# Query copies on VectorE, and two block pairs of tiles 3 to 6 by seven products, in an attention and feed-forward kernel

## The chip, the cores and the metric

The kernel runs on one core of one Trainium2 chip. The metric is the device time of one execution in microseconds (us), the median over several runs. Engines: TensorE (PE, its weight loads PEld), VectorE (DVE), ScalarE (ACT), GpSimd (POOL) and SyncE (SP).

## The reference

Attention with two kinds of mask, 8 batches, 8 heads, 576 positions, head size 64, then a bilinear feed-forward over all 4608 tokens of 512 features:

```python
scores = (1.0 / np.sqrt(D)) * np.matmul(q, k.transpose(0, 1, 3, 2))
rel = pos[:, None] - pos[None, :]
mask_local = (rel >= 0) & (rel < 32)
mask_strided = (rel >= 0) & (pos[None, :] % 32 == pos[:, None] % 32)
# heads 0-3 take mask_local, heads 4-7 mask_strided; masked scores are -1e9
attn = softmax(scores); o = np.matmul(attn, v)
x = o.transpose(0, 2, 1, 3).reshape(4608, 512)
out = ((x @ w_a) * (x @ w_b)) @ w_out        # w_a, w_b: 512 x 1536, w_out: 1536 x 512
```

## The kernel before, in words

**Feed-forward.** The 4608 tokens are nine tiles `t` = 0 to 8 of 512 tokens. A tile has 16 slots. Slots 0 to 11 are the blocks `f` of 128 of the 1536 inner features (`ffn_ab`): four matmuls of 512 columns for a = x @ w_a, four for b = x @ w_b (`ab_mm`, L612), a copy of a from PSUM by ScalarE (L633), and the product a * b by VectorE into `pf` (L636). Slots 12 to 15 are the y part, the multiplication with w_out. From tile 1 on it runs by seven products instead of eight (`products`, L816), whose sums of `pf` VectorE makes beforehand (`fast_s`, L750, called `ps`). The activations `xT` are a ring of four batches of 576 columns; in tile 4 the ring's end falls in the middle of the tile, and its matmuls are cut into two of 256 columns.

**Block pairs by seven products.** Seven products of half-size blocks give the four quarters of a (two feature blocks by two token halves) that eight would otherwise give. Before the change this is done for a in five pairs of tile 7 and six of tile 8 (`FAST_A`, `a_pair`), a pair being blocks 2g and 2g+1; b stays ordinary. A product is two matmuls of 256 columns (L689). Products 1, 6, 5 and 3 add up, one after the other, in one PSUM bank X; after each, ScalarE copies X into one quarter of a (L705, L708, L716, L724). Bank Z holds products 7 and 4, bank Y product 2, and they are added to the quarters by VectorE or GpSimd. The matmuls of b (L696) stand between the products. Sums of weights (`wsum_make`, L653) and differences of x (`xsum_make`, L663) are made beforehand by VectorE, the weight sums in tile 6.

**Attention.** It runs one tile ahead: batch b's steps are handed out over the slots of tile b-1 by tables (`STEPS` for batches 1 and 2, `LATER` and `IN_Y` for 3 to 7); a position of .5 is in the middle of a slot, between a and b. Each batch has eight units u, two for each of four pairs of heads c: units 0 to 3 are local heads, 4 to 7 strided heads.
- `Q`: copies the transposed queries `qT` of one half of the partitions j into the zero-padded query tile `qz` (`step_Q`, L333 strided, L335 local; GpSimd). Q0 and Q1 are the local heads, Q2 and Q3 the strided ones. `step_D` issues the transposing DMAs into `qT` on SyncE's queue.
- `S`: score matmuls (`S_p`, L377), exponential on ScalarE (L397), mask on VectorE (`S_m`, L415).
- `V`: output matmuls into the PSUM tile `o` of two banks. For the local heads (`V_p`, L454) VectorE takes reciprocals and scales (L462, L480); for the strided ones (`step_VT`, L513) ScalarE takes logarithm and exponential (L523, L524) and VectorE scales into `xT` (L527).
- `O`, `I`: the local heads' outputs go to DRAM and come back transposed into `xT`.

**Order.** Each engine's order is the program's order, written out by hand: a slot's matmuls, copy and product, then `take(i)`, the attention steps of the position, then `at[i]`, the other work put down for the slot with `do` (loads, sums, transposes). Ahead of `at[i]`, GpSimd copies one element of the slot's result (`pace`, L1054), so that the loads it issues keep pace.

**PSUM.** Eight banks: two for scores `st`, two for `o`, three `mm` and one `tp`, which `mm_bank` hands out in turn to the blocks and the y part.

Of the kernel before, what the change touches and what calls it, by code (L numbers as in the profile page):

```python
# [7 lines left out]
F32 = mybir.dt.float32  # L8
BF16 = mybir.dt.bfloat16
I16 = mybir.dt.int16  # L10
ALU = mybir.AluOpType
# [14 lines left out]
WCH = (0, 2, 5, 9, 12)  # L26
FAST_Y = (1, 2, 3, 4, 5, 6, 7, 8)
FAST_A = {7: (1, 2, 3, 4, 5), 8: (0, 1, 2, 3, 4, 5)}


@with_exitstack
def kernel(
# [34 lines left out]
    def open_psum(stack, **bufs):  # L67
        for nm, n in bufs.items():
# [7 lines left out]

    qz_pair = [(const.tile([128, 2, 2, S], BF16, name=f"qz{i}l"), const.tile([128, 2, RS, 2, NP], BF16, name=f"qz{i}s"))
               for i in range(2)]
    qz_buf = [[(l[:, :, j], s[:, :, :, j]) for j in range(2)] for l, s in qz_pair]
    qz_flat = [[l.rearrange("p a b c -> p (a b c)"), s.rearrange("p a b c d -> p (a b c d)")] for l, s in qz_pair]  # L80
# [29 lines left out]
    def fill_v(t):  # L110
        nc.gpsimd.memset(t[:, :, :, D:] if len(t.shape) == 4 else t[:, :, D:], 1.0)

# [65 lines left out]
    tl = {}  # L178

    def blocks(nm, z):  # L180
        z = int(z)
        return sb.tile([128, 2, (S, RS * GP)[z]], BF16, tag=f"t{nm}{z}", name=f"t{nm}{z}", bufs=1)

# [142 lines left out]
    def step_Q(b, z, j):  # L326

        r = slice(64 * j, 64 * j + 64)
        src = qT[z][r]
        if z:  # L330
            src = src.rearrange("d (c h p i) -> d c h i p", c=2, h=2, i=4)
            for c in range(2):
                nc.gpsimd.tensor_copy(qz_buf[b % 2][j][1][r, c].rearrange("d (h i) p -> d h i p", h=2), src[:, c])  # L333
        else:
            nc.gpsimd.tensor_copy(qz_buf[b % 2][j][0][r], src)  # L335

# [21 lines left out]
    def S_p(b, u):  # L358
# [5 lines left out]
        if b > 0:  # L364
            sv = st.rearrange("p a (i n) -> p (a i) n", n=256)
            for i in range(G):
                k0 = (G * half + i) * (LW if c < 2 else GP)
                if c < 2:
                    rhs = qz_pair[b % 2][0][:, c % 2, :, k0:k0 + n]
                else:  # L370
                    rhs = qz_pair[b % 2][1][:, c % 2, G * half + i]
                if c < 2 or b < FIRST_D:
                    lhs = kT[:, c % 2, k0:k0 + 128]
                else:
                    k0 = W * (u - HL) + i
                    lhs = kT_strided(b)[:, k0:k0 + 509:4]
                nc.tensor.matmul(sv[:, i, :2 * n].rearrange("p (j n) -> p j n", j=2), lhsT=lhs, rhs=rhs, start=True, stop=True)  # L377
            return
# [48 lines left out]
    def V_p(b, u):  # L427
# [11 lines left out]
        else:  # L439
            o = psum4["o"].tile([128, 2, 512], F32, tag="o", name="o")  # L440
            of = o[:, :, :G * (D + 1)].rearrange("p j (g e) -> p j g e", e=D + 1)
            sm = of[:, :, :, D:]
# [59 lines left out]
    def step_VT(b, u):  # L502

        c, half, M, n, G = unit(u)
        p = ps.pop((b, u))
        o = psum4["o"].tile([128, 2, 512], F32, tag="o", name="o")
        for i in range(G):
            for j in range(2):
                if c < 2:
                    vt = vl_buf[b % 2][:, (2 * c + j) * 6 + 3 * half + i]  # L510
                else:
                    vt = vs_buf[b % 2][:, u - HL, 2 * i + j]
                nc.tensor.matmul(o[:, j, i * n:(i + 1) * n], lhsT=vt, rhs=p_cols(b, p, j, i, n, n)[:M], start=True, stop=True)  # L513
# [40 lines left out]
    def step_X(b, c):  # L554
# [17 lines left out]
                 12.6: "S1", 12.75: "L0 X2", 13: "s2 X3 V0 m2 L1 W3", 13.5: "V1 S3", 14: "V2 X0", 14.5: "V3", 15: "X1"},  # L572
             2: {16.5: "Q0 Q1", 20: "S0 Q2", 20.5: "S1", 21: "V0 Q3", 21.5: "S2", 22: "V1", 22.5: "S3 O0", 23: "V2", 23.5: "S4",
                 24: "V3 I0 O1", 24.5: "S5", 25.5: "V4", 26: "S6", 26.5: "I1", 27: "V5", 27.5: "S7", 28.5: "V6", 30: "V7"}}
    LATER = {-6: "Q0", -5: "Q1", -1: "S0", 0: "S1", 1: "V0 Q2", 2: "S2", 3: "V1 O0 Q3", 4: "S3 I0", 5: "V2", 6: "S4", 7: "V3 O1", 8: "S5", 9: "V4 I1",
             10: "S6",
# [38 lines left out]
    def ffn_ab(t, f, mid, ab=None):  # L615
        if f == 0:
            pfs[t] = fsb.tile([128, FD, TTOK], BF16, tag="pf", name="pf", bufs=1)
        pf = pfs[t]
        if f // 2 in FAST_A.get(t, ()):
            if f % 2 == 0:  # L620
                pairs[t, f // 2] = a_pair(t, f // 2)
            return next(pairs[t, f // 2])
        if ab is None:
# [6 lines left out]
            else:  # L630
                ab_mm(t, f, ab, range(KD), mid)
        a_sb = fsb.tile([128, TTOK], F32, tag="a_sb", name="a_sb")
        nc.scalar.copy(a_sb, ab[0])  # L633
# [3 lines left out]
        else:  # L637
# [3 lines left out]
    wav = wa_sb.rearrange("p (j c) (g e m) -> p j c g e m", c=2, e=2, m=128)  # L641
    wsum_a = [flat.rearrange("p (c g m) -> p c g m", c=2, g=FG)
              for flat in [vl_buf[0].rearrange("p a b -> p (a b)")[:, 12 * 128 * z:12 * 128 * (z + 1)] for z in range(2)]
              + [t[:, :12 * 128] for t in qz_flat[0]]]
    xsum = {t: qz_flat[1][t - 7][:, :8 * HT].rearrange("p (n c m) -> p n c m", n=4, c=2)
            for t in FAST_A}

    def wsum_make(n):
        w, s_ = (lambda e, j: wav[:, j, :, :, e]), wsum_a
        a, b, op = ((w(1, 0), w(1, 1), ALU.add), (s_[0], w(0, 0), ALU.subtract), (w(0, 0), w(1, 0), ALU.subtract),  # L650
                    (w(0, 1), s_[1], ALU.subtract))[n]
        for c in range(2):
            nc.vector.tensor_tensor(s_[n][:, c], a[:, c], b[:, c], op=op)  # L653

    def x_part(t, j, k):
        x0 = TTOK * t % (XR * S) + HT * k
        return xT[:, 2 * j:2 * j + 2, x0:x0 + HT]
# [7 lines left out]
    pairs = {}  # L665

    def a_pair(t, g):

        pf = pfs[t]
        pool, nm = ((pst, "st"), (psum4["o"], "o"))[g % 2]  # L670
        X = pool.tile([128, 2, 512], F32, tag=nm, name="ax")[:, 0, :HT]
        a = ([fsb.tile([128, TTOK], F32, tag="a_sb", name="a_sb") for _ in range(2)] if g % 2 == 0 else
             [t.rearrange("p h n -> p (h n)")[:, :2 * TTOK].bitcast(F32) for t in kT_buf[0]])
# [62 lines left out]
    later = {}  # L736

    pss = {}

# [88 lines left out]
    def y_tail(t):  # L828

        plan, y = products(t), y_bufs()  # L830
        banks = {("X", 1): psum4["o"].tile([128, 2, 512], F32, tag="o", name="end")[:, 0, :HN],
                 ("Z", 1): pst.tile([128, 2, 512], F32, tag="st", name="end")[:, 0, :HN]}
# [74 lines left out]
    with tc.manual_schedule(engines={ENG.PE, ENG.SP, ENG.Pool, ENG.DVE, ENG.Activation}):  # L907
# [71 lines left out]
        early.close()  # L979
        open_psum(ctx, mm=3, tp=1, o=1)  # L980
        slots = []
        for t in range(NT):
# [22 lines left out]
        for b in range(FIRST_D, B):  # L1005
            g0 = 16 * (b - 2)
            if b == FIRST_D:
                do(0, load_qk, b, False)
                do(1, load_qk, b, True)
                do(15, load_vl, b)  # L1010
                for h in range(HL):
# [10 lines left out]
        for n in range(4):  # L1022
            do(16 * (NT - 3) + 2 * n + 2, wsum_make, n)
        do(16 * (NT - 2) - 1, xsum_make, NT - 2, 0)
# [8 lines left out]
        for i, jz in ((14, (0, 0)), (14, (1, 0)), (15, (0, 1)), (15, (1, 1))):  # L1033
            do(i, zero_qz, 0, nc.gpsimd, (jz,))
        do(28, fill_v, vs_buf[1])
        for n, slot in enumerate((16, 16, 19, 20)):
# [51 lines left out]
```

## Time and profile before

| | before |
|---|---|
| median of 3 runs | 326.83 us (326.56 to 326.98) |
| the profiled execution | 326.64 us |
| its span, first to last instruction | 324.9 us |
| TensorE busy | 315.5 us, 97% of the span |
| VectorE busy | 234.1 us, 72% |
| ScalarE busy | 186.4 us, 57% |
| GpSimd busy | 150.1 us, 46% |
| tile 3, 128.3 to 161.7 us: TensorE, VectorE, ScalarE, GpSimd busy | 33.24, 24.26, 19.92, 16.65 us |
| one a copy, 128x512 (L633) | 585 ns, 84 of them |
| one product a * b, 128x512 (L636) | 684 ns, 74 of them |
| one query copy on GpSimd: local 64x1152 (L335); strided, half of it (L333) | 1.15 us median, 12 of them; 0.70 us, 24 of them |

The span is the time on the core; the rest of an execution's time lies around it. A matmul's own duration includes the way through the array, so matmuls that follow each other overlap: 512 columns last 379 ns, and the next starts 216 ns later. What a stretch costs TensorE is read from the starts. In a timeline row the columns are: start, duration, engine, line, operation, written tile <- read tiles, shape, count, and in brackets the idle time before it and what ended that.

### The profile page before, as it was taken

The page shows a single profiled execution, that of the slowest core. Times are in us where ns is not written, and L with a number is a line of the kernel's source. Part 1 is how long each engine was busy: PE and PEld are TensorE (multiplying, and loading weights), DVE is VectorE, ACT ScalarE, POOL GpSimd, SP SyncE. Part 2 cuts the span into 40 slices and gives each one's busy share as a digit, 9 for nine tenths or more (in the row PEclk, how much of TensorE's full clock was granted, in tenths as well). Part 3 has the DMA queues.
Part 4 walks back from the last instruction along what each step waited for, and adds up shares of the span by engine and source line. Part 5 has one row for each costly group of instructions (what it writes and reads, how often), then busy time and mean ns, then how long its engine had stood idle before and what let it go on. Part 6 is the DMA issues. An engine that isn't in the chain of part 4 may idle for free.

```text
span 324.9 us, 7111 instructions
## 1 busy us (share of the span) xinstructions
PE 315.5 (97%) x2706; PEld 214.2 (66%) x2734; DVE 234.1 (72%) x489; ACT 186.4 (57%) x331; POOL 150.1 (46%) x240
## 2 busy tenths in 40 slices
PE   8999999998999999999999999999999999999994
PEld 6754555454765578556999995559555866786684
DVE  6765786498956785688667766777699667857862
ACT  6763766454754476447644765467546655535541
POOL 8944922893785356524652565336124003202520
PEclk9999999999999999999999999999999999999998
DMA  8999999999699999999998999999863030004004
GB/s 150 155 204 196 204 187 204 204 126 175 87 132 153 191 129 101 131 207 167 102 104 181 158 107 107 158 182 112 59 101 103 2 113 17 3 2 129 0 3 129
DMA packets 127234, 40.40 MB, mean 124 GB/s; under 512 B 115040, under 2 KB 124320, under 8 KB 127008
## 3 DMA queue, kind: packets, MB, share of 16 engines
q0 software_dynamic: 80400, 19.28, 64.5%
q1 hardware_dynamic: 46656, 20.61, 36.3%
q8 instruction: 21, 0.34, 0.5%
q14 instruction: 13, 0.11, 0.1%
q10 hardware_dynamic: 144, 0.07, 0.1%
HBM read 39.12 MB, written 18.28 MB: 177 GB/s over the span
## 4 chain that ended last, share of the span: by engine, by line
PE 89%; DVE 4%; ACT 2%; issue 2%; DMA 2%; POOL 0%; ACTq 0%; POOLq 0%
PE mm L612 42%; PE mm L816 18%; PE mm L696 5%; PE st L377 4%; PE mm L878 3%; PE ax L689 3%; PE o L454 2%; PE mm L689 2%; PE o L513 2%; DMA shared<-in_q_dram 2%; PE mm L843 2%; PE end L843 1%; DVE p L415 1%; PE misc L156 1%; PE tp L540 1%
## 5 line engine op out<-in xcount | busy, mean ns | idle before, releaser
L612 PE MATMUL mm<-xT,wb_sb 128*128 128x512 bf16 (+1 forms) x381 | 88.0, 352 | 0.4
L612 PE MATMUL mm<-xT,wa_sb 128*128 128x512 bf16 (+1 forms) x367 | 86.6, 351 | 0.6
L633 ACT COPY a_sb<-mm 128x512 f32<-128x512 f32 x84 | 49.2, 585 | 47.1 <-PE mm L612 45.5
L636 DVE TENSOR_TENSOR pf<-a_sb,mm 128x512 bf16<-128x512 f32 x74 | 50.6, 684 | 26.0 <-PE mm L612 18.4
L612 PEld LDWEIGHTS <-wb_sb 128*128 128x128 bf16 x392 | 37.8, 98 | 33.7 <-issue 0.4
L1054 POOL CAST pace<-pf 1x1 f32<-1x1 bf16 x72 | 21.0, 291 | 77.0 <-DVE pf L636 47.8
L612 PEld LDWEIGHTS <-wa_sb 128*128 128x128 bf16 x392 | 34.9, 98 | 20.9
L397 ACT ACTIVATE p<-st 72x576 bf16<-72x576 f32 (+1 forms) x56 | 36.4, 650 | 20.1 <-PE st L377 19.8
L816 PEld LDWEIGHTS <-ps 128*128 128x128 bf16 x336 | 32.5, 98 | 4.6 <-issue 0.5
L527 DVE TENSOR_TENSOR xT<-o,xr 64x576 bf16<-64x576 f32 x24 | 18.0, 751 | 19.8 <-ACT xr L524 19.6
L816 PE MATMUL mm<-wf,ps 128*128 128x256 bf16 x252 | 30.1, 273 | 0.5 <-ACT y_sb L781 0.3
L781 ACT COPY y_sb<-mm 128x512 f32<-128x512 f32 (+1 forms) x32 | 17.9, 559 | 19.3 <-PE mm L816 16.6
L816 PEld LDWEIGHTS <-pf 128*128 128x128 bf16 x252 | 23.6, 98 | 2.7
L696 PE MATMUL mm<-xT,wb_sb 128*128 128x512 bf16 x83 | 25.3, 379 | 0.1
L816 PE MATMUL mm<-wo_sb,pf 128*128 128x256 bf16 x168 | 21.8, 273 | 0.0
L750 DVE TENSOR_TENSOR ps<-pf 128x512 bf16<-128x512 bf16 (+1 forms) x49 | 21.2, 433 | 0.7
L523 ACT ACTIVATE xr<-o 64x576 f32<-64x576 f32 x24 | 15.6, 648 | 9.4 <-PE o L513 9.2
L1054 POOL COPY pace<-y_sb 1x1 f32<-1x1 f32 x17 | 4.1, 241 | 36.0 <-ACT y_sb L887 13.3
L236 POOL DMA_DIRECT2D vs<-in_v_dram x24 | 20.4, 863 | 0.0
L415 DVE TENSOR_TENSOR p<-p,mask_s 72x576 int16<-72x576 int16 x28 | 18.7, 669 | 1.8 <-ACT p L397 1.5
L454 PEld LDWEIGHTS <-p 128*128 128x128 bf16 (+1 forms) x256 | 13.0, 97 | 8.9 <-DVE xl L480 2.1
L415 DVE TENSOR_TENSOR p<-p,mask_l 128x576 int16<-128x576 int16 x32 | 14.7, 458 | 4.3 <-ACT p L397 4.3
(183 smaller groups left out, 546.7 us busy)
## 6 DMA issues: line engine op xcount, KB each, us to landing
out_dram<-y_sb SPq DMA_DIRECT2D x14, 512.0 KB, 4.9
kr<-in_k_dram POOLq DMA_DIRECT2D x12, 288.0 KB, 5.8
qr<-in_q_dram POOLq DMA_DIRECT2D x12, 288.0 KB, 6.9
vl<-in_v_dram POOLq DMA_DIRECT2D x6, 384.0 KB, 9.5
out_dram<-y_sb SPq DMA_DIRECT2D x7, 256.0 KB, 4.1
vs<-in_v_dram POOLq DMA_DIRECT2D x24, 72.0 KB, 5.9
xd<-xl SPq DMA_DIRECT2D x12, 144.0 KB, 4.8
wo_sb<-in_moe_w_out_dram POOLq DMA_DIRECT2D x4, 384.0 KB, 10.4
```

The lines of the kernel that those rows point to most:

```text
L236: nc.gpsimd.dma_start(out=vs_buf[b % 2][:, h, :, 0:D], in_=v[b, HL + h].rearrange("(p r) d -> p r d", r=RS))
L397: nc.scalar.activation(p_flat(p)[:M, :2 * W].rearrange("p (i n) -> p i n", n=2 * n), st[:M].rearrange("p a (i n) -> p (a i) n", n=256)[:, ...
L415: nc.vector.tensor_tensor(pi, pi, mk, op=ALU.bitwise_and)
L454: nc.tensor.matmul(of[:, j, i, :w], lhsT=pt, rhs=vt, start=True, stop=True)
L527: nc.vector.tensor_mul(dst.rearrange("d (p i j) -> d p i j", i=G, j=2), o[:64, :, :W].rearrange("d j (i p) -> d p i j", p=NP), r)
L612: nc.tensor.matmul(ps_[:, c0:c0 + n], lhsT=w[:, kk, 128 * f:128 * (f + 1)], rhs=xT[:, kk, x0:x0 + n], start=(kk == first and c0 == 0), sto ...
L633: nc.scalar.copy(a_sb, ab[0])
L636: nc.vector.tensor_mul(pf[:, f, :].rearrange("p (i a s) -> p a i s", i=2, s=16), halves(a_sb), halves(ab[1]))
L696: nc.tensor.matmul(got[e], lhsT=wb_sb[:, kk, 128 * f:128 * (f + 1)], rhs=xT[:, kk, x0:x0 + TTOK], start=kk == 0, stop=kk == KD - 1)
L750: nc.vector.tensor_tensor(s[:, n], a, b, op=op)
L816: nc.tensor.matmul(bank[b][:, q], lhsT=lhs(g, q), rhs=rhs(g), start=k in "172" and q == 0 and g == 0, stop=g == FG - 1, skip_group_check=True)
L1054: nc.gpsimd.tensor_copy(pace, done)
```

## The change

1. `step_Q` copies on VectorE instead of GpSimd, and copies plainly: the strided query tile keeps the order of `qT`, and the score matmuls of the strided heads (batches 2 to 7) read it with a step of four elements. The positions of the Q steps move: batch 2's from 16.5, 16.5, 20 and 21 to 18, 19, 22.5 and 23; later batches' from -6, -5, 1 and 3 to -4, -3, 2 and 4.
2. In tiles 3 to 6 the pairs g = 1 and 3 (blocks 2, 3 and 6, 7) compute a by seven products (`MID_A`, `a_pair_mid`). X is the second bank of the attention outputs. `o` becomes one tile for the whole run, `o_psum`; V0 to V3 put their outputs into its first bank alone, and `step_VT` fills the first bank before the second.
3. The weight sums, now in the staging tiles of early batches (made larger), move from tile 6 to tile 2, one half in a slot; the differences of x for tiles 3 to 6 get a tile of their own and are made in the slot before the tile and in its first. The a copies have three buffers instead of two.
4. `fill_v` leaves out the column that is set already, and moves for the second v tile from slot 28 to slot 2; one load of v moves from slot 15 to 14.

The core of the diff:

```diff
+MID_A = {t: (1, 3) for t in (3, 4, 5, 6)}
 FAST_A = {7: (1, 2, 3, 4, 5), 8: (0, 1, 2, 3, 4, 5)}
...
-(const.tile([128, 2, 2, S], BF16, name=f"qz{i}l"), const.tile([128, 2, RS, 2, NP], BF16, name=f"qz{i}s"))
+(const.tile([128, 2, 2, S], BF16, name=f"qz{i}l"), const.tile([128, 2, 2, RS, NP], BF16, name=f"qz{i}s"))
...
     def step_Q(b, z, j):
         r = slice(64 * j, 64 * j + 64)
-        src = qT[z][r]
-        if z:
-            src = src.rearrange("d (c h p i) -> d c h i p", c=2, h=2, i=4)
-            for c in range(2):
-                nc.gpsimd.tensor_copy(qz_buf[b % 2][j][1][r, c].rearrange("d (h i) p -> d h i p", h=2), src[:, c])
-        else:
-            nc.gpsimd.tensor_copy(qz_buf[b % 2][j][0][r], src)
+        dst = qz_buf[b % 2][j][z][r]
+        nc.vector.tensor_copy(dst.rearrange("d c r n -> d (c r n)") if z else dst, qT[z][r])
...
                     lhs = kT_strided(b)[:, k0:k0 + 509:4]
+                    rhs = qz_pair[b % 2][1].rearrange("p j c r n -> p j (c r n)")[:, :, k0:k0 + 4 * NP - 3:4]
...
-            o = psum4["o"].tile([128, 2, 512], F32, tag="o", name="o")
-            of = o[:, :, :G * (D + 1)].rearrange("p j (g e) -> p j g e", e=D + 1)
+            of = o_psum[:, 0, :2 * G * (D + 1)].rearrange("p (j g e) -> p j g e", j=2, e=D + 1) if c < 2 else (
+                o_psum[:, :, :G * (D + 1)].rearrange("p j (g e) -> p j g e", e=D + 1))
...
-             2: {16.5: "Q0 Q1", 20: "S0 Q2", 20.5: "S1", 21: "V0 Q3", 21.5: "S2", 22: "V1", 22.5: "S3 O0", 23: "V2", 23.5: "S4",
+             2: {18: "Q0", 19: "Q1", 20: "S0", 20.5: "S1", 21: "V0", 21.5: "S2", 22: "V1", 22.5: "S3 O0 Q2", 23: "V2 Q3", 23.5: "S4",
...
-    LATER = {-6: "Q0", -5: "Q1", -1: "S0", 0: "S1", 1: "V0 Q2", 2: "S2", 3: "V1 O0 Q3", 4: "S3 I0", 5: "V2", 6: "S4", 7: "V3 O1",
+    LATER = {-4: "Q0", -3: "Q1", -1: "S0", 0: "S1", 1: "V0", 2: "S2 Q2", 3: "V1 O0", 4: "S3 I0 Q3", 5: "V2", 6: "S4", 7: "V3 O1",
...
+    def a_pair_mid(t, g):
+        pf = pfs[t]
+        X = o_psum[:, 1, :HT]
+        Y, Z, b1, b0 = [mm_bank([128, TTOK]) for _ in range(4)]
+        Y, Z = Y[:, :HT], Z[:, :HT]
+        a = [fsb.tile([128, TTOK], F32, tag="a_sb", name="a_sb", bufs=3) for _ in range(2)][::-1]
+        p7 = fsb.tile([128, HT], F32, tag="p7", name="p7")
...
+        P(Y, w(0, 1), x(1, 0), True)                 # product 2
+        b_mm(b1, 1, (0, 1))
+        P(X, w(0, 0), x(0, 0), True)                 # product 1
+        nc.scalar.copy(quarter(0, 0), X)
+        b_mm(b1, 1, (2, 3))
+        P(X, ws(1), xs(1))                           # product 6
+        nc.scalar.copy(quarter(1, 0), X)
+        P(Z, ws(2), xs(2), True)                     # product 7
+        nc.scalar.copy(p7, Z)
+        add(quarter(0, 0), Y)
+        yield p7[:1, :1]                             # end of the even slot: its attention steps follow
+        P(X, ws(0), xs(0))                           # product 5
+        nc.scalar.copy(quarter(1, 1), X)
+        b_mm(b0, 0, (0,))
+        P(Z, w(1, 1), xs(3))                         # product 4
+        add(quarter(1, 0), Z)
+        add(quarter(1, 1), p7)
+        b_mm(b0, 0, (1, 2, 3))
+        P(X, ws(3), x(1, 1))                         # product 3
+        nc.scalar.copy(quarter(0, 1), X)
+        mult(1, b1)
+        mult(0, b0)
+        yield pf[:1, 2 * g, :1]
...
         for n in range(4):
-            do(16 * (NT - 3) + 2 * n + 2, wsum_make, n)
+            for c in range(2):
+                do(16 * 2 + (2, 5, 7, 9, 11, 13, 14, 15)[2 * n + c], wsum_make, n, c)
+        for t in MID_A:
+            do(16 * t - 1, xsum_make, t, 0)
+            for n in (1, 2, 3):
+                do(16 * t, xsum_make, t, n)
```

(The comments with the products' numbers are added here.) `add` and `mult` are VectorE operations: an addition of 256 columns, and the product a * b of 512.

## The prediction

> **What bounds the kernel now.** I read the page first, then the chain that ended last, then the timeline of the three stretches that the change touches. The sum below is made against the profiled execution: 326.64 us, of which 324.9 us are span; the median of the runs shown is 326.83 us, 0.19 us more, and 0.2% of it (0.65 us) is about what a measurement of this kernel can tell from no change.
>
> The page's busy line and its chain:
> ```profile
> PE 315.5 (97%) x2706; PEld 214.2 (66%) x2734; DVE 234.1 (72%) x489; ACT 186.4 (57%) x331; POOL 150.1 (46%) x240
> ...
> PE 89%; DVE 4%; ACT 2%; issue 2%; DMA 2%; POOL 0%; ACTq 0%; POOLq 0%
> ```
> TensorE is the bound: a saving counts only in TensorE's order, and a new wait there counts in full. Tiles 3 to 6 take some 33.4 us each and TensorE is busy 33.24 of 33.40 us in tile 3 (table by stretches), so there is no idle time there to hide a wait in.
>
> Tile 7 already has block pairs by seven products, without attention beside them. Its timeline, from the start of one pair to the start of the next:
> ```profile
> 266.10 0.38 PE L689 MATMUL ax<-xT,wa_sb 128*128 128x256 bf16 x2
> ...
> 266.32 0.81 PE L696 MATMUL mm<-xT,wb_sb 128*128 128x512 bf16 x3
> 266.52 0.37 ACT L705 COPY kT0l<-ax 128x256 f32<-128x256 f32 x1 [0.50 <-PE ax L689]
> ...
> 266.97 0.38 PE L689 MATMUL ax<-qz1l,vl 128*128 128x256 bf16 x2
> ...
> 269.36 0.38 PE L689 MATMUL ax<-xT,wa_sb 128*128 128x256 bf16 x2
> ```
> A pair takes 3.26 us. The two products in bank X show the loop that the new code has too: product, ScalarE copy, next product onto the same bank. The first product's matmuls start at 266.10, the copy at 266.52, it ends at 266.89, and the second product starts at 266.97, just when the three 512-column matmuls between them are through. So no wait is seen, but the margin is 0.08 us.
>
> The first attention steps on transposed queries (tile 1):
> ```profile
> 70.42 2.04 DVE L750 TENSOR_TENSOR ps<-pf 128x512 bf16<-128x512 bf16 x1
> ...
> 70.67 1.50 POOL L333 COPY qz0s<-qTs 64x576 bf16<-64x576 bf16 x2
> ...
> 74.18 0.35 PE L454 MATMUL o<-vl,p 128*128 128x65 bf16 x6 [1.07 <-DVE xl L480]
> ...
> 75.24 0.41 PE L377 MATMUL st<-qz0s,kT0s 128*128 128x144 bf16 x4
> ...
> 83.17 1.52 DVE L415 TENSOR_TENSOR p<-p,mask_s 72x576 int16<-72x576 int16 x1
> 83.24 1.14 POOL L335 COPY qz1l<-qTl 64x1152 bf16<-64x1152 bf16 x1
> ```
> A VectorE operation with both inputs in SBUF that meets a GpSimd copy lasts until the copy is over: 2.04 us where its kind takes 0.42, 1.52 where others take 0.45. In tile 1 VectorE has no slack, and TensorE waits 1.07 us for it. Later copies meet masks too (1.52 us at 117.46, 151.13, 185.00 and 218.71), but no wait of TensorE there reaches 0.1 us.
>
> **The products.** A matmul of 512 columns starts 0.216 us after the one before (8 in 1.73 us), one of 256 columns 0.109 us (84 in 9.18 us). Two ordinary blocks are 16 x 0.216 = 3.46 us. A pair is 8 x 0.216 for b and 14 x 0.109 for a: 3.25 us, the 3.26 of tile 7. Saved: 0.20 us a pair, 0.22 in tile 4, where the ring's end cuts all its matmuls in halves (16 x 0.109 = 1.75 a block). Two pairs in four tiles: 6 x 0.20 + 2 x 0.22 = 1.64 us off TensorE.
>
> What they add is waits in the chain of bank X. From the first matmul of a product to that of the next onto the same bank it takes 0.11 (second matmul's start) + 0.27 (its duration) + 0.04 (to the copy) + 0.37 (the copy) + about 0.05 (an end to a waiting matmul: copy end 89.81, matmul 89.86) = 0.84 us. TensorE's own work in between, counted with the product:
> - product 1 to product 6: 0.22 + two matmuls of b, 0.43 = 0.65. Wait 0.19 us. (Tile 7 has three of them, 0.87.)
> - product 6 to product 5: 0.22 + product 7, 0.22 + the score matmuls of S2 or S4 that stand there, 0.25 (next line) = 0.69. Wait 0.15 us. (Tile 7 has 0.87 here as well.)
> - product 5 to product 3: 0.22 + 0.22 + 0.22 + 0.65 = 1.31, against 0.84 and the exponential of 0.65 us that stands ahead of the copy on ScalarE; that exponential starts some 0.3 us before product 5 is done, so the sum comes out between 0 and 0.1 us. I take 0.
>
> ```profile
> 133.58 0.41 PE L377 MATMUL st<-qz0l,kT0l 128*128 128x192 bf16 x3
> ...
> 133.83 1.03 PE L612 MATMUL mm<-xT,wa_sb 128*128 128x512 bf16 x4
> ```
> The score step delays the next block by 0.25 us.
>
> Per pair 0.34 us of waiting for 0.20 saved. Eight pairs: 2.72 - 1.64 = **+1.1 us**. Bounds: if the pass from copy to matmul cost nothing, 8 x 0.24 - 1.64 = +0.3; with 0.1 at the third place, +1.9. That the waits vanish altogether is a rival below.
>
> Bank 1 of the attention outputs is free for X in those slots: V0 to V3 now use bank 0 alone, and V7 in the y part of the tile before is scaled at 128.11, product 1 of tile 3 stands at about 132.5.
>
> **VectorE and ScalarE under the pairs.** A pair adds three 256-column additions on VectorE (0.42 each, rows L713 and L722) and swaps two 0.585 us copies on ScalarE for five of 0.37. The x differences (four of 0.42 a tile) and the queries (below) come on top. VectorE's 16.85 us in tile 3's 23.3 us of blocks become 16.85 - 0.5 (mask no longer held up in that window) + 2.5 + 1.3 + 0.9 = 21.0, 90%. I cost this at nothing: a product bank is asked for again two blocks later, some 2.6 us after its last matmul, and the y part of the tile (VectorE 7.4 of 10.1 us) takes up the lag. If that cover is gone, each 0.1 us of lag beyond it costs 0.1 us a pair. The weight sums move from tile 6 to tile 2, eight of 0.51 to 0.55 (two in 1.02); tile 2's VectorE has 24.27 of 33.60 us, so nothing. The wider staging tiles, the a copy in three buffers and the earlier fill of the v tile (1.82 us of GpSimd, at a time when its queue has no successor for 10 us) cost nothing for the same kind of reason. Third waits of VectorE: a query copy waits at its head for the transpose, with masks and products behind it. In tile 2 that DMA landed at 100.00 and VectorE gets there after the mask at 101.04; in the other tiles the margin is about 2 us or more.
>
> **The query copies.** 24 GpSimd copies (12 of 1.15 us, 24 halves of 0.70) go; 24 VectorE copies of 64x1152 come. Nearest rows, plain bf16 copies:
> ```profile
> 40.44 1.04 DVE L269 COPY tq<-shared 96x768 bf16<-96x768 bf16 x1
> 41.40 0.27 DVE L240 COPY vs<-tk 72x512 bf16<-72x512 bf16 x1
> 41.97 0.34 DVE L269 COPY tq<-shared 96x768 bf16<-96x768 bf16 x1
> ```
> 0.27 for 512 and 0.34 for 768 give about 0.45 us for 1152 (estimate); 1.04 is a copy that ran while GpSimd was issuing DMAs. I take 0.45 and keep 1.04 as the upper end. In tiles 2 to 6 they have slack: Q2 and Q3 stand two slots (3.9 us) ahead of S4.
>
> In tile 1 they have none. There Q3 stands behind V2, half a slot ahead of S4, which reads it. Without the collision VectorE's order there runs (each start one pipelined interval after the last): sum at 70.4, mask of S2 70.8, product f6 71.2, V1's reciprocal and scaling 71.8 to 72.6, sum 72.5, mask of S3 73.0 (its exponential ends 72.93), Q2 73.4, product f7 73.8, V2's pair 74.4 to 75.1, Q3 75.1 to 75.5. V2's matmuls now need no wait (72.6 against 73.1), so TensorE is through block 8's first half at 74.0 and then waits for Q3 until 75.6. Before, S4 started at 75.24: 0.35 us later than before, not earlier. The wait moves from V2 to S4. In the y part of tile 1 two waits of 0.17 us (a sum, and V6 behind the scaling of V5) follow the masks that were held up; I let them go: -0.34. Sum for tile 1: **0**, from -1.4 (1.07 and 0.34 go, nothing comes) to +1.4 (Q2 and Q3 at 1.04).
>
> **The strided reading.** S4 to S7 now read the queries as moving operand with a step of 4 elements: 6 batches x 4 units x 4 = 96 matmuls of 144 columns, 0.061 us apart. No row has a stepped moving operand. The nearest is the weight load with the same step, 113 ns (kT0s) against 98 (kT0l): 15% more, which here would be 0.9 us; half speed would be 5.8 us; nothing is the other end. I take 0, since in the rows the stepped load is closest to the plain one. The Trainium skill, page "SBUF — State Buffer", section "Door 1: The DMA port swizzle", says that a step up to 8 bf16 elements is free as two accesses still share a 16-byte line; by it the term is 0, too, and the half-speed case is excluded. No run here shows it yet.
>
> **Sum.** +1.1 (pairs) + 0 (tile 1) + 0 = 326.64 + 1.1 = 327.7 in the profiled execution, 327.9 against the median.
>
> **Rivals.**
> - *The chain of X doesn't bind* (faster). If a product needed only as long as the gaps in the code give, 0.65 and 0.69, all 1.64 us are saved, and if in addition tile 1's 1.07 + 0.34 are recovered: 326.8 - 3.0 = 323.8; with half of it, 325.3. For it: tile 7 shows pairs at full pace, and VectorE's hold-ups are real. Against it: copy end minus first matmul is 0.79 in tile 7, above both gaps. It decides as soon as the wait at product 6 is under 0.1 us. 0.14.
> - *No difference.* One of the two waits in a pair is covered (S2 or S4 waiting on something that would have waited anyway) or tile 1 gains what the pairs lose: about 326.8. 0.16.
> - *VectorE's copies are held up by GpSimd's DMA issue.* At 1.04 us each, tile 1 loses 1.2 more and tiles 3 to 6 0.2 each, as VectorE then falls behind block 4's second bank: 327.9 + 2.0 = 329.9. For it the 1.04 row; against it the other copies of the same kind, at 0.27 to 0.35 among DMA issues. The Trainium skill, page "SBUF — State Buffer", section "SBUF: two separate sides", has the same mechanism as a rule: such a copy and any GpSimd operation exclude each other, first come first served. By that rule it happens where a GpSimd operation is already running. 0.12.
> - *The change doesn't do what it says:* bank 1 is handled as one with bank 0, so that X waits for V0's and V2's scaling (133.31 for a product at 132.5 in tile 3): 8 x 0.8 or more, 334; or the stepped reading runs at half speed, 333.7. 0.05.
> - The forecast, waits of 0.2 to 0.5 us a pair: 0.53.
>
> **Numbers.** Forecast 327.9. Left out of the range: the full gain (down to 323.8, most of 0.14) and the 0.05; it runs from 326.2 to 330.4. Faster 0.15, within 0.2% 0.17, slower 0.68.
>
> **What would show it.** Right: in tiles 3 to 6 the product after the first copy starts 0.84 us after the first product, with TensorE's idle time put down to ScalarE's copy, 0.1 to 0.2 us twice a pair, and pairs with their score step some 0.15 us longer than two blocks with theirs; masks of the strided heads all at 0.45; in tile 1 a wait of over 1 us at S4 for VectorE's copy into qz0s. Wrong: pairs at 3.25 us beside attention; query copies far from 0.45; gaps over 0.061 us between the score matmuls of S4 to S7; or waits of TensorE for VectorE in tiles 3 to 6.

## The result and the profile after

The changed kernel takes 348.65 us (348.64 to 349.25, four runs) where the kernel before takes 326.9 (four runs beside it): 1.0668 times the time, 95% interval 1.065 to 1.0687. The forecast was 327.9, slower; the direction came out, the size, 21.8 us instead of 1.1, did not. Ratios below leave out runs disturbed by a low granted clock, as ten of e10's twelve were (0.984 to 0.993 in the mean), so that its ratio stands below what its median says.

The busy line and the chain of the page of after:

```profile
PE 324.1 (93%) x2738; PEld 222.6 (64%) x2766; DVE 250.9 (72%) x553; ACT 189.6 (55%) x355; POOL 121.1 (35%) x211
...
PE 77%; DVE 8%; ACT 5%; POOL 5%; issue 3%; DMA 2%; ACTq 0%; POOLq 0%; DVEq 0%
```

TensorE's share of the chain fell from 89 to 77%. VectorE, ScalarE and GpSimd, 6% before, stand for 18%: TensorE now waits for them. Its waits (engine and line that waited, for what; total us, times, longest us):

```profile
PE o L684 <- DVE xl L481: 7.6, 8, 1.0
PE o L455 <- ACT a_sb L727: 3.7, 8, 0.5
PE st L378 <- DVE qz0s L335: 1.5, 1, 1.5
PE st L378 <- POOL pace L1125: 1.3, 1, 1.3
```

Two of them come eight times, once in each new pair: a product (L684) waits for VectorE's scaling of attention outputs, and output matmuls (L455) wait for ScalarE's last copy out of X. The first pair of tile 3 in the timeline shows both:

```profile
134.59 0.34 PE L455 MATMUL o<-vl,p 128*128 128x65 bf16 x6
...
134.78 0.38 PE L684 MATMUL mm<-xT,wa_sb 128*128 128x256 bf16 x2
...
135.00 0.59 PE L698 MATMUL mm<-xT,wb_sb 128*128 128x512 bf16 x2
...
136.02 0.55 DVE L481 TENSOR_TENSOR xl<-o,rc 96x384 bf16<-96x384 f32 x1
136.62 0.38 PE L684 MATMUL o<-xT,wa_sb 128*128 128x256 bf16 x2 [1.03 <-DVE xl L481]
...
137.04 0.37 ACT L711 COPY a_sb<-o 128x256 f32<-128x256 f32 x1 [2.52 <-PE o L684]
...
137.46 0.38 PE L684 MATMUL o<-xsum,tq 128*128 128x256 bf16 x2
...
139.65 0.38 PE L684 MATMUL o<-xT,tq 128*128 128x256 bf16 x2
...
140.07 0.37 ACT L727 COPY a_sb<-o 128x256 f32<-128x256 f32 x1 [0.67 <-PE o L684]
...
140.50 0.34 PE L455 MATMUL o<-vl,p 128*128 128x65 bf16 x6 [0.46 <-ACT a_sb L727]
```

Product 1 writes the second bank of `o_psum`, V0's outputs lie in the first, and yet it starts 0.05 us after VectorE has read the first one (136.57). V1 writes the first bank and starts just after X, in the second, has been copied (140.44). From starts, TensorE loses 136.62 - 135.43 = 1.19 us at the first place and 140.50 - 139.87 = 0.63 at the second; the bracket shows 0.16 less, since a matmul's duration runs on after its columns are in. That is 1.82 us in this pair. In the second pair of the tile, where no x difference stands ahead of the scaling, the first wait is 0.87 us by its bracket, 1.03 from starts. All eight pairs together: 7.6 + 3.7 us of brackets and 0.16 more at each of 16 places, 13.9 us.

Tile 1 in the timeline, and the score matmuls by form:

```profile
62.77 1.63 POOL L212 DMA_DIRECT2D kr<-in_k_dram  x1 [0.23 <-issue]
...
63.51 2.80 DVE L335 COPY qz0l<-qTl 64x1152 bf16<-64x1152 bf16 x1
...
63.88 2.15 POOL L212 DMA_DIRECT2D qr<-in_q_dram  x1
...
66.92 0.47 DVE L335 COPY qz0l<-qTl 64x1152 bf16<-64x1152 bf16 x1
...
67.54 0.41 PE L378 MATMUL st<-qz0l,kT0l 128*128 128x192 bf16 x3 [1.29 <-POOL pace L1125]
...
76.25 0.46 DVE L335 COPY qz0s<-qTs 64x1152 bf16<-64x1152 bf16 x1
76.86 0.68 PE L378 MATMUL st<-qz0s,kT0s 128*128 128x144 bf16 x4 [1.54 <-DVE qz0s L335]
```
```profile
L378 PE MATMUL st<-qz1s,kT1s x64: 226/308/319, 33.8 to 276.1; 128*128 128x144 bf16 x64
...
L378 PE MATMUL st<-qz0l,kT0l x36: 243/246/246, 67.5 to 219.6; 128*128 128x192 bf16 x36
```

S4 waits 1.54 us for Q3, as forecast; S0 waits 1.29, which was not. The first query copy took 2.80 us while GpSimd issued loads; of the 23 after it one took 0.63 us, the others 0.44 to 0.47. S0 reads what the second copy wrote, which came behind the first on VectorE and ended at 67.39; the bracket names GpSimd's `pace`, which ended 0.04 us later. And a strided score unit takes 0.68 us where it took 0.41: worked out from these rounded rows, its matmuls follow each other after (0.68 - 0.308) / 3 = 0.124 us instead of (0.41 - 0.226) / 3 = 0.061; the starts in the traces give 0.130 and 0.063, as medians.

### The profile page after: what moved, and what is told of

It is laid out like the page before. It is cut to its first block, busy times and chain, and to the rows that moved or that the text cites. A ratio compares the mean times of both kernels' runs of the same rounds, so it can differ in the third digit from the quotient of the medians.

```text
span 346.9 us, 7227 instructions
## 1 busy us (share of the span) xinstructions
PE 324.1 (93%) x2738; PEld 222.6 (64%) x2766; DVE 250.9 (72%) x553; ACT 189.6 (55%) x355; POOL 121.1 (35%) x211
## 4 chain that ended last, share of the span: by engine, by line
PE 77%; DVE 8%; ACT 5%; POOL 5%; issue 3%; DMA 2%; ACTq 0%; POOLq 0%; DVEq 0%
PE mm L613 27%; PE mm L881 17%; PE st L378 5%; PE mm L760 5%; PE o L684 3%; DVE pf L637 3%; PE mm L698 2%; PE o L455 2%; PE mm L943 2%; PE mm L753 2%; DMA vl<-in_v_dram 2%; PE o L514 2%; PE o L753 2%; PE mm L908 2%; DVE xl L481 1%
## 5 line engine op out<-in xcount | busy, mean ns | idle before, releaser
L613 PE MATMUL mm<-xT,wb_sb 128*128 128x512 bf16 (+1 forms) x301 | 71.7, 356 | 0.4
L613 PE MATMUL mm<-xT,wa_sb 128*128 128x512 bf16 (+1 forms) x287 | 70.4, 356 | 0.6
L634 ACT COPY a_sb<-mm 128x512 f32<-128x512 f32 x68 | 39.7, 584 | 34.9 <-PE mm L613 33.4
L1125 POOL CAST pace<-pf 1x1 f32<-1x1 bf16 x68 | 17.4, 256 | 101.3 <-DVE pf L637 49.7
L613 PEld LDWEIGHTS <-wb_sb 128*128 128x128 bf16 x312 | 30.2, 98 | 27.7 <-issue 0.4
L637 DVE TENSOR_TENSOR pf<-a_sb,mm 128x512 bf16<-128x512 f32 x58 | 39.5, 681 | 10.3 <-ACT a_sb L634 5.8
L613 PEld LDWEIGHTS <-wa_sb 128*128 128x128 bf16 x312 | 28.7, 99 | 18.2
L1125 POOL COPY pace<-y_sb 1x1 f32<-1x1 f32 x21 | 9.3, 443 | 48.7 <-DVE y_sb L844 23.3
L881 PE MATMUL mm<-wo_sb,pf 128*128 128x256 bf16 x168 | 21.8, 273 | 0.0
L455 PEld LDWEIGHTS <-p 128*128 128x128 bf16 (+1 forms) x256 | 13.3, 97 | 11.3 <-issue 5.9
L815 DVE TENSOR_TENSOR ps<-pf 128x512 bf16<-128x512 bf16 (+1 forms) x49 | 19.6, 400 | 0.8
L416 DVE TENSOR_TENSOR p<-p,mask_s 72x576 int16<-72x576 int16 x28 | 12.7, 453 | 9.6 <-ACT p L398 9.5
```

What stands on the lines that cost most here:

```text
L416: nc.vector.tensor_tensor(pi, pi, mk, op=ALU.bitwise_and)
L455: nc.tensor.matmul(of[:, j, i, :w], lhsT=pt, rhs=vt, start=True, stop=True)
L613: nc.tensor.matmul(ps_[:, c0:c0 + n], lhsT=w[:, kk, 128 * f:128 * (f + 1)], rhs=xT[:, kk, x0:x0 + n], start=(kk == first and c0 == 0), sto ...
L637: nc.vector.tensor_mul(pf[:, f, :].rearrange("p (i a s) -> p a i s", i=2, s=16), halves(a_sb), halves(ab[1]))
L815: nc.vector.tensor_tensor(s[:, n], a, b, op=op)
L881: nc.tensor.matmul(bank[b][:, q], lhsT=lhs(g, q), rhs=rhs(g), start=k in "172" and q == 0 and g == 0, stop=g == FG - 1, skip_group_check=True)
```

## The experiments

Theory A: two prices that the sum put at nothing or left to a rival, the two banks of `o_psum` waited for as one, and the step in the reading. Theory B: VectorE has too much to do. The last column is the time from tile 3's first block matmul to tile 7's in the profiled run, a measure free of the start of the kernel, which varies: in these profiled runs tile 1 begins at 57.05 to 60.86 us. Each ratio is to runs of the kernel before that were made beside the kernel in question, with medians of 326.12 to 326.9 us.

| kernel | median us | ratio to before, 95% interval | tiles 3 to 6, us |
|---|---|---|---|
| before | 326.9 | | 134.68 |
| after | 348.65 | 1.0668, 1.065 to 1.0687 | 153.73 |
| e1 pairs only | 349.56 | 1.0705, 1.0649 to 1.0761 | 157.22 |
| e2 queries only | 334.96 | 1.0251, 1.0221 to 1.0282 | 139.07 |
| e3 step 1 | 343.07 | 1.0509, 1.0476 to 1.0541 | 150.18 |
| e4 step 2 | 343.57 | 1.0509, 1.0461 to 1.0558 | 150.35 |
| e12 step 3 | 346.11 | 1.059, 1.0543 to 1.0638 | 151.93 |
| e5 two tiles | 334.14 | 1.0235, 1.0205 to 1.0265 | 139.56 |
| e11 pairs, late copies | 343.41 | 1.0523, 1.0474 to 1.0571 | 150.89 |
| e6 pairs, two tiles | 327.97 | 1.0046, 1.0019 to 1.0073 | 135.77 |
| e7 pairs, two tiles, cover | 325.53 | 0.9968, 0.9942 to 0.9994 | 134.24 |
| e9 the same, copies on VectorE | 326.61 | 0.9996, 0.997 to 1.0023 | 133.04 |
| e10 the same, batch 2 spread | 332.28 | 0.9956, 0.991 to 1.0002 | 133.10 |
| e13 the same, batch 2 on GpSimd | 325.13 | 0.9952, 0.9928 to 0.9975 | 133.05 |
| e14 strided copies on VectorE | 325.49 | 0.9963, 0.9936 to 0.9991 | 133.05 |

### Half of the change each: e1 and e2

e1 puts `step_Q`, its layout and its positions back to before and leaves the pairs; e2 leaves the queries and takes the pairs out.

```diff
-MID_A = {t: (1, 3) for t in (3, 4, 5, 6)}     # e2
+MID_A = {}
```

> The block pairs and the one-tile attention outputs alone; the query copies are back on GpSimd, in the old layout and at the old positions, and the score matmuls read without a step. Theory A (two prices: the step costs 0.27 us in each of 24 score units, and X waits for the scaling of V0 to V3 and V1/V3 wait for X's copies, as the two banks are one tile): 348.65 - 6.5 for the step - about 0.7 for tile 1 = 341.5 us, tiles 3 to 6 at about 37.1 us each, TensorE's waits for L481's line and X's copies unchanged. Theory B (VectorE is too loaded by query copies and additions, and TensorE waits for it): 24 copies less, so the waits at the pairs shrink to half or less, below 336 us.

> The query copies on VectorE with the stepped reading, no pairs in tiles 3 to 6 (the weight sums stay in tile 2). Theory A: 326.9 + 24 x 0.27 for the step + about 0.7 (tile 1: two new waits of 1.3 and 1.5 us at S0 and S4 against those of 1.07 and 0.34 that go) = 334.1 us, each tile from 2 to 6 longer by 1.1 us. Theory B: VectorE has slack without the pairs, so about 328 us.

e2 came out at A's number: the query half alone costs 2.5%, 8.2 us. 24 score units at 0.27 us are 6.5 of them. Tile 1 gives 1.0 more: it takes 38.67 us instead of 36.57, with its four score units in the difference (1.08), for waits of 1.3 us at S0 and 1.5 at S4 where there were 1.4 in all before. The remaining 0.7 us is less than the start of the kernel varies by. e1 missed A's number as well as B's, by 8 us or more. Its trace shows why its waits are longer than in the changed kernel (waits, then the timeline of tile 3):

```profile
PE o L688 <- DVE xl L485: 11.7, 8, 2.3
PE o L459 <- ACT a_sb L731: 3.7, 8, 0.5
```
```profile
130.84 1.74 POOL L338 COPY qz0s<-qTs 64x576 bf16<-64x576 bf16 x2
...
131.11 0.93 DVE L672 TENSOR_TENSOR xsum<-xT 128x512 bf16<-128x512 bf16 x1
...
131.97 0.91 DVE L672 TENSOR_TENSOR xsum<-xT,xsum 128x512 bf16<-128x512 bf16 x1
...
134.22 0.38 PE L688 MATMUL o<-xT,wa_sb 128*128 128x256 bf16 x2 [2.04 <-DVE xl L485]
```

The x differences stand ahead of V0's scaling on VectorE, and beside GpSimd's copy two of them last 0.93 and 0.91 us instead of 0.42. X waits for that scaling, so each such delay reaches TensorE. e11 puts it to the test: the same kernel with the copies of batches 3 to 7 at the positions of the changed kernel, past the x differences.

```diff
-    LATER = {-6: "Q0", -5: "Q1", -1: "S0", 0: "S1", 1: "V0 Q2", 2: "S2", 3: "V1 O0 Q3", 4: "S3 I0", ...
+    LATER = {-4: "Q0", -3: "Q1", -1: "S0", 0: "S1", 1: "V0", 2: "S2 Q2", 3: "V1 O0", 4: "S3 I0 Q3", ...
```

> The first experiment's kernel (pairs alone, one tile of two banks, GpSimd's permuting copies, no step in the scores), with the query copies at the places of the changed kernel, so that GpSimd's copy of slot 1 no longer stands beside VectorE's x sums, ahead of the scaling that X waits for. Theory C (the copies beside the x sums made those waits longer, 2.04 us at tile 3's first pair against 1.03 in the changed kernel): that wait comes back to about 1 us, TensorE's waits for the scaling fall from 11.7 us to about 8, and the time to about 346 us. Theory D (the excess over 341.5 us is the lower granted clock alone, 0.96 in tiles 4 and 6): waits as they were, and 349 us.

The waits for the scaling fell to 8.3 us, the one in tile 3 to 1.03, and the ratio from 1.0705 to 1.0523: theory C, with a time 2.6 us under the one it named. In tile 6 one copy still meets an x difference, which then lasts 1.68 us (243.40), and the wait behind it is 2.30. Of e1's 6.3 us more in tiles 3 to 6, its two tiles at full granted clock are 1.02 and 1.28 us longer than e11's. The rest lies in tiles 4 and 6, where e1 was granted 0.96 of the clock; why it was, these runs don't tell.

### The step: e3, e4, e12

Only the columns that S4 to S7 read are other ones:

```diff
-rhs = ...[:, :, k0:k0 + 4 * NP - 3:4]
+rhs = ...[:, :, W * (u - HL) + NP * i:W * (u - HL) + NP * (i + 1)]     # e3; e4 and e12: steps of 2 and 3
```

> The changed kernel, but the score matmuls of the strided heads read 72 neighbouring query columns instead of every fourth (other columns, so the scores are of other queries); copies, waits and counts of instructions are the same. Theory A: the four matmuls of a unit are 0.061 us apart again instead of 0.15, 24 x 0.27 = 6.5 us less, 342.1 us. Theory B, and the rule that a step of 8 bytes is free: 348.6 us, the longer row being something else, such as a wait.

> The changed kernel, with the queries of the strided heads read at a step of 2 elements instead of 4 (other columns, so other scores; 144 columns out of a stretch of 576 bytes instead of 1152). At a step of 4 a score matmul of 144 columns follows the one before after about 0.15 us, at a step of 1 after 0.061. Theory A1, any step costs the same because each column is then fetched by itself: score units stay at 0.68 us and the time at 348.6 us. Theory A2, the price goes with the stretch of bytes that is walked through (1152 bytes in 0.15 us): 0.075 us at a step of 2, units of some 0.45 us, and 344 us. Theory A3, up to a step of 2 nothing: 0.41 us a unit and 343 us, as with a step of 1.

> The changed kernel with the queries of the strided heads read at a step of 3 elements (other columns, so other scores): the size between the step of 2 that was free (units of 0.41 us, 343.6 us) and the step of 4 that was not (0.68 us, 348.65). Theory A1, half speed as soon as a column is further than 4 bytes from the one before: 0.68 us a unit and 348.6 us. Theory A2, a price that grows with the step: some 0.54 us a unit and 346 us.

The score matmuls by form, in e3, e4 and e12 (duration min/median/max in ns):

```profile
L378 PE MATMUL st<-qz1s,kT1s x64: 226/226/226, 33.5 to 270.4; 128*128 128x144 bf16 x64
```
```profile
L378 PE MATMUL st<-qz1s,kT1s x64: 224/228/233, 33.4 to 270.7; 128*128 128x144 bf16 x64
```
```profile
L378 PE MATMUL st<-qz1s,kT1s x64: 226/262/269, 33.6 to 273.3; 128*128 128x144 bf16 x64
```

Units of four take 0.41, 0.43, 0.56 and 0.68 us at steps of 1, 2, 3 and 4, which by the same working as above is one matmul after 0.061, 0.067, 0.099 and 0.124 us; the medians of the starts are 0.063, 0.067, 0.097 and 0.130. (The 0.15 in e4's expectation is too much: it left out that the single matmul is longer, too.) Up to 2 elements there is next to no price; from there it grows with the step (e12: the second theory), and at 4 the speed is half. e3 took 5.6 us off the changed kernel's median, which is theory A; it named 6.5, but beside the pairs a part of S4's longer time falls into the wait of product 5.

### The banks: e5 and e6

`o_psum` becomes two tiles of one bank each; what read or wrote both banks in one VectorE or ScalarE instruction (the strided units) now takes two.

```diff
-o_psum = psum4["o"].tile([128, 2, 512], F32, tag="o", name="o")
+o_psum = [psum4["o"].tile([128, 512], F32, tag=f"o{j}", name=f"o{j}") for j in range(2)]
...
-        X = o_psum[:, 1, :HT]
+        X = o_psum[1][:, :HT]
```

e5 is the changed kernel with this; e6 is that with the query half taken out, that is, the pairs as the prediction priced them.

> The changed kernel with the attention outputs as two tiles of one bank each; V4 to V7 (and batch 1's) scale each bank by an operation of its own, one more on ScalarE and on VectorE per unit. Theory A: X no longer waits for V0's and V2's scaling, nor V1 and V3 for X's last copy: the 11.3 us of TensorE's waits that the profile lists there, and some 0.16 us more for each of 16, go: 334.8 us, with waits of 0.1 to 0.2 us left in the chain of X. Theory B: VectorE's load is a little higher, so 348.6 us or more.

> Pairs alone: query copies on GpSimd in the layout, at the places and with the plain reading of the kernel before, and the attention outputs in two tiles of one bank instead of one tile of two, so that X waits for nothing that V0 to V3 leave in the other bank. This is the pair as the prediction priced it. Theory A (the chain of X is all that is left): waits of 0.1 to 0.2 us twice a pair for a saving of 0.20, +1.1 us: 327 to 328 us, with TensorE's waits in tiles 3 to 6 put down to ScalarE's copies. GpSimd's copies may hold up VectorE's x sums beside it, up to 1 us more. Theory B (VectorE is overloaded by sums, additions and multiplications in 256 columns): waits for VectorE in tiles 3 to 6 and 331 us or more. If the chain does not bind: 325 us.

e5's waits begin with

```profile
PE st L378 <- DVE qz0s L335: 1.5, 1, 1.5
PE st L378 <- POOL pace L1127: 1.3, 1, 1.3
```

and both waits that came eight times are gone: 14.2 us less in tiles 3 to 6, with everything else left in, though VectorE got more instructions (585 against 553). That settles A against B. e6 came out at the forecast's own number, and its timeline shows the forecast's chain, product 1, 6, 5, 3:

```profile
133.58 0.38 PE L690 MATMUL o<-xT,wa_sb 128*128 128x256 bf16 x2
...
134.42 0.38 PE L690 MATMUL o<-xsum,tq 128*128 128x256 bf16 x2
...
134.86 0.41 PE L382 MATMUL st<-qz0l,kT0l 128*128 128x192 bf16 x3
...
135.26 0.38 PE L690 MATMUL o<-xsum,tk 128*128 128x256 bf16 x2
...
136.56 0.38 PE L690 MATMUL o<-xT,tq 128*128 128x256 bf16 x2
```

Starts 0.84, 0.84 and 1.30 us apart, where TensorE's own work is 0.65, 0.69 and 1.31.

### Towards a kernel that beats both: e7, e9, e10, e13, e14

e7 is e6 with tile 7's order of work in the pair, so that product 6 is covered:

```diff
-        P(Y, w(0, 1), x(1, 0), True)
-        b_mm(b1, 1, (0, 1))
         P(X, w(0, 0), x(0, 0), True)
         nc.scalar.copy(quarter(0, 0), X)
-        b_mm(b1, 1, (2, 3))
+        b_mm(b1, 1, (0, 1, 2))
         P(X, ws(1), xs(1))
         nc.scalar.copy(quarter(1, 0), X)
+        b_mm(b1, 1, (3,))
         P(Z, ws(2), xs(2), True)
         nc.scalar.copy(p7, Z)
+        P(Y, w(0, 1), x(1, 0), True)
```

> As the kernel with pairs alone and two tiles of one bank, but with the order of work inside a pair that tile 7 has: product 1, three matmuls of b, product 6, one matmul of b, product 7, product 2. TensorE's own work between products 1 and 6 is then 0.87 us, as much as the chain of X needs (0.84). Theory A: the wait at product 6 goes, 8 x 0.19 = 1.5 us less than without the cover; 326 us, about the kernel before. Theory B (VectorE): no difference between the two.

Tiles 3 to 6 lost 1.53 us, for the 8 x 0.19 expected, but that the two agree is luck, as tile 3 shows:

```profile
130.52 1.68 DVE L674 TENSOR_TENSOR xsum<-xT,xsum 128x512 bf16<-128x512 bf16 x1
130.59 1.33 POOL L338 COPY qz0s<-qTs 64x576 bf16<-64x576 bf16 x2
...
131.10 0.38 PE L690 MATMUL o<-xT,wa_sb 128*128 128x256 bf16 x2
...
132.26 0.39 PE L690 MATMUL o<-xsum,tq 128*128 128x256 bf16 x2
```

In the second pair of each tile product 6 starts 0.86 to 0.88 us after product 1. In the first pair it starts 1.14 to 1.17 after, since it reads an x difference that, beside GpSimd's strided query copy, lasts 1.68 or 1.69 us instead of 0.42 and has just ended (132.20). Product 5 now stands behind product 2 as well and starts 1.12 to 1.13 us after product 6, more than the 0.84 of the chain, so that its wait is gone, too. Both waits gone are 8 x 0.34 = 2.7 us less; 4 x 0.29 for the late x differences takes 1.2 of it back.

e9 is e7 with the query copies on VectorE, at the changed kernel's positions, the strided ones permuting, so that no score reads with a step. A half of 64x576 so permuted lasts 0.45 us, as long as a plain copy of 64x1152: twice the price for the same data.

> The changed kernel without its two hidden prices and with the cover: attention outputs in two tiles of one bank, tile 7's order inside the pairs, query copies on VectorE as in the change, but the ones of the strided heads as permuting copies into the layout of before (two halves of 64x576 with a step of 4 in the source), so that the scores read without a step. Theory A: it differs from the kernel with cover and GpSimd copies only in tile 1 (waits of 1.3 us at S0 and 1.5 at S4 for VectorE, against 1.1 at V2) and by what the permuting copies cost VectorE (0.45 to 0.9 us each, twelve): 326 to 329 us. Theory B (VectorE): 330 us or more, with TensorE waiting for VectorE in tiles 3 to 6.

In tiles 3 to 6 the whole saving came out, 1.64 us, but tile 1 gave it back: 1.30 us at S0 and 1.91 at S4. e10 spreads batch 2's copies over three engines to free VectorE there.

```diff
+        if b == 2 and z and j:
+            copy = nc.scalar.copy
+        else:
+            copy = (nc.gpsimd if b == 2 and not z else nc.vector).tensor_copy
```

> The kernel with two tiles of one bank, cover and permuting VectorE copies, with batch 2 handled apart, since tile 1 has no slack on VectorE: its long-window copies go back to GpSimd at their old place (they met GpSimd's DMA issue on VectorE and cost 1.30 us at S0), its strided ones stand half a slot earlier, one on VectorE, the other on ScalarE (S4 waited 1.91 us for them). In the kernel it starts from, tiles 3 to 6 took 133.04 us against 134.68 before. Theory A: these 1.64 us stay, and tile 1 waits 0 to 1 us in all, no more than the 1.4 of before: 324 to 325.3 us. Theory B (VectorE is short in tile 1 whatever the order): some 2 us of waits remain there, 326 us.

```profile
PE mm L623 <- DMA xT<-xd: 4.9, 1, 4.9
PE o L465 <- DVE xl L500: 1.1, 1, 1.1
```

The waits at S0 and S4 are gone, one of 1.1 us stands at V3 instead, and a new wait of 4.9 us stands at the head of tile 2: the outer outputs' write (xd) was issued at 86.74 us, and the transposing read behind it not before 92.93. In e9 these were 82.42 and 84.63. After it the granted clock is 0.95 in tile 2. The wait need not come in every execution: the profiled one took 330.4 us, the shortest of the twelve 324.0, within theory A's range, and there is no trace of that one. GpSimd's loads start earlier here than in e7 (keys and queries at 71.22 instead of 73.89 us, values at 83.06 instead of 84.33), since no copies stand ahead of them; that they hold up the write is argued, not shown.

e13 puts all of batch 2's copies back on GpSimd, e14 also the local ones of the later batches, each at its position of before.

```diff
+        copy = (nc.gpsimd if b == 2 else nc.vector).tensor_copy               # e13
+        copy = (nc.gpsimd if b == 2 or not z else nc.vector).tensor_copy      # e14
```

> The kernel with two tiles of one bank, cover and permuting VectorE copies, but batch 2's query copies on GpSimd at their places of before. Tiles 3 to 6 should take 133.0 us (1.64 less than before) as in the kernel it starts from, and tile 1 should wait some 1.1 us at V2, as before. Theory A: 324.3 us. Theory T (transfers): GpSimd no longer copies batch 3's queries at slots -6 and -5, its queue runs on, the loads of values behind those copies start 1 to 2 us sooner, and the write of the outer outputs (xd) lands late again, as where the wait for xT took 4.92 us: 326 us or more.

> The kernel with pairs, cover and GpSimd copies, and of the query copies only those of the strided heads from batch 3 on given to VectorE (slots 2 and 4 of tiles 2 to 6, where they stood beside VectorE's x sums and masks). GpSimd's queue in tile 1 and the loads behind it stay as they were. Theory A (GpSimd's copies beside the x sums and masks are why tiles 3 to 6 take 134.24 us there and 133.04 with VectorE copies): 133 to 133.5 us in tiles 3 to 6, 324.5 us in all. Theory E (all six kinds of GpSimd copies matter, the long ones in the y part too): 134 us, 325.3 us.

Both keep tiles 3 to 6 at 133.05 us, 1.63 less than before. So it is the strided copies, beside the x differences, that cost e7 its 1.2 us there, and theory E falls. The medians are 0.8 and 1.0 us above what theory A named for each. The wait for xT is 0.4 and 0.6 us in these two, although e13 too has no copies of batch 3 ahead of the loads of values: theory T, as put, falls. The earlier loads of keys and queries were not tried by themselves, and the cause of e10's 4.9 us stays open. e13 is the fastest in median, 0.5% under the kernel before; neither e14 nor e7 can be told from it by the time of the whole. The pairs of e13 in the timeline of tile 3:

```profile
131.84 0.39 PE L691 MATMUL o<-xT,wa_sb 128*128 128x256 bf16 x2
...
132.07 0.81 PE L705 MATMUL mm<-xT,wb_sb 128*128 128x512 bf16 x3
...
132.71 0.38 PE L691 MATMUL o<-xsum,tq 128*128 128x256 bf16 x2
```

Product 6 starts 0.87 us after product 1, right behind three matmuls of b, as in tile 7.

## Why the prediction was wrong, and where it was right

Tiles 3 to 6 can be added up from the table: 134.68 before; + 4.39 for the step (e2; 16 units at 0.27); + 0.49 for the pairs (e5); + 14.17 for the shared tile (after). That is 153.73. Tile 2, which took in the weight sums, lost nothing by them: 33.67 us before and in e3, where no score reads with a step.

**"Bank 1 of the attention outputs is free for X in those slots": the step that failed, some 14 us.** The prediction asked whether anything in the second bank was in use at that time, and nothing was. But X and V's outputs were parts of one tile, and each waited for the whole of it, in both directions (e5). The rival "the change doesn't do what it says" named this with a chance of 0.05, together with the half speed below, as one or the other; both came. Its price was too small as well: "8 x 0.8 or more", from V0's scaling as the kernel before had it, against 14.17 / 8 = 1.77 a pair. In the first pair of a tile the x differences now stand ahead of that scaling on VectorE (1.19; 1.03 in the second pair), and V1 or V3 waits for X's last copy (0.63), which the rival left out.

**"The strided reading. I take 0": failed, 5.6 us by e3.** The bounds given (0, 0.9, 5.8) held that at their far end, and the 6.5 us that the step costs without the pairs (e2) lies beyond it. The value was taken from the weight load with the same step, 15% longer: the nearest row, but of weights and not of a moving operand. The Trainium skill, page "SBUF — State Buffer", section "Door 1: The DMA port swizzle", has a step of up to 8 bf16 as free; for the moving operand of a matmul that nearly holds here at a step of 2 (0.067 us for 0.063) and not at 3 and 4 (0.097 and 0.130), and the measurement decides.

**Tile 1, taken at 0 from -1.4 to +1.4: mis-sized by some 1.0 us, within its bounds.** Tile 1 took 38.66 us instead of 36.57; 1.08 of that is the step in its four score units. The shift from V2 to S4 came as worked out (wait over 1 us, 1.54 measured). What was left out is the first query copy at its new place, under GpSimd's load issue: 2.80 us, and S0 late by 1.29. The rival "held up by GpSimd's DMA issue" had the mechanism and placed it in the same tile at 1.2 us; in tiles 3 to 6, where it expected 0.2 each, the copies took 0.44 to 0.46. The Trainium skill, page "SBUF — State Buffer", section "SBUF: two separate sides", describes such an exclusion; the 2.80 us and e1's 0.93 agree with it, the copies that ran at their usual 0.45 us beside short load issues (last section) don't.

**The pairs, +1.1: right, as the sum stood.** e6 measured +1.07 in the median and +1.09 in tiles 3 to 6, with the 0.84 us of the chain at both places in all eight pairs and nothing at the third, so the mechanism is right with the number. In the changed kernel itself the pairs cost 0.49: the slower score unit S4 gives TensorE 0.27 us more to do between products 6 and 5, and covers that wait (0.15) in four of the eight pairs. The rival "the chain of X doesn't bind" was wrong for this order and right for tile 7's: there all 1.64 us come out as soon as no GpSimd copy holds up the x differences (e9, e13, e14).

**VectorE and ScalarE at nothing: held, once the tile was split** (e5 has no wait for VectorE in tiles 3 to 6). With the shared tile the same queue cost 1.19 us in the first pair of a tile and 1.03 in the second, since X then waited for an operation far behind in it. Masks at 0.45 us and copies at 0.45: as forecast.

## What to carry to other kernels

A second bank is free only if it is free as the program sees it: where two users share one tile, each waits for the other's last access, so give the new user a tile of its own, and before believing that a bank is free, name the object that is waited on. The price of a step in one kind of operand is not read from a row of another kind, and a small test of one size decides it. A saving that comes out at the forecast's number can still be the sum of two others (e7): look at the starts in each place before calling it shown. When two forecasts of the same rival can both be true, add them up once, and look for what new work stands in the queue ahead of the operation waited for.

## What was not expected of the hardware

- A bf16 moving operand of TensorE read with a step of 1, 2, 3 and 4 elements: 0.063, 0.067, 0.097 and 0.130 us for 144 columns (medians of the starts in e3, e4, e12 and the changed kernel).
- On VectorE a copy of 64x576 bf16 whose source has a step of 4 takes 0.45 us, as long as a plain 64x1152 (e9).
- One VectorE copy took 2.80 us under GpSimd's load issue (62.77 to 66.03 us) where its kind takes 0.45; others beside shorter load issues (for example the one at 139.54, with issues of about 0.5 us each at 139.18 and 139.67) were not longer at all.
- The granted clock was 0.96 in tiles 4 and 6 of e1 and 0.95 in tile 2 of e10. The clock records of the traces hold the loss in one piece each: 0.5 for 3.4 us, from 174.1 and 252.6 us in e1, 1.2 and 0.7 us after waits of 2.28 and 2.30 us ended, and from 99.0 in e10, 0.2 us after the wait of 4.92. e11 had a wait of 2.30 us, too (247.09), and no such piece, so a link with the waits is likely but not shown.
